# First Gram stage of a delta-rule attention kernel: zero fills and mask casts on ScalarE, sums of squares a step ahead, first keys fetched by two queues

One core of one Trainium2 chip. The metric is the device time of one execution in microseconds (us). All ratios below are the mean time of one kernel's fast runs over the mean of the other's fast runs of the same rounds, so they are not quite the ratios of the medians that stand beside them.

## What is computed

```python
# deltanet: B, H, S, D = 4, 8, 768, 48
k_n = k / (norm(k, axis=-1) + 1e-6)
for t in range(S):
    y[:, :, t] = q[:, :, t] @ state
    v_old = state^T @ k_n[:, :, t]
    state += beta[t] * outer(k_n[:, :, t], v[:, :, t] - v_old)
# then, on x = y as [3072, 384]:
h = x @ w_in                                     # d_ff = 2048
out = (max(h, 0) + alpha * min(h, 0)) @ w_out
```

The kernel cuts the sequence into chunks of 64. A "step" is one such chunk of two of the four sequences, all heads; for each step it needs the products of the keys among each other (the Gram matrices), and for four steps at a time VectorE inverts the resulting triangular blocks ("elimination"). The feed-forward part is TensorE's work and takes most of the time; `alpha` holds its "slopes".

## The kernel before: the parts that matter

```python
def squares(n):                      # sums of squares of the keys of step n
    ksq = work.tile([128, H, D], FP32, name="ksq", bufs=1)
    nc.scalar.square(ksq, early(n)[:, :, 0:D])
    nc.vector.tensor_reduce(out=norm, in_=ksq, axis=AXX, op=ALU.add)

def weigh(n):
    nc.scalar.sqrt(norm, norm)
    nc.vector.tensor_scalar_add(norm, norm, 1e-6)          # L324
    nc.vector.reciprocal(rec, norm)
    nc.gpsimd.tensor_tensor(...)                           # two small products
    ...
def statics(first, last):            # Gram stage of some steps
    for n in range(first, last + 1):
        prep(n)                      # squares(n), weigh(n)
        flips(n, N)                  # transposes of the keys on TensorE
        yield
        ...
            grams(n - 1, N)          # Gram products, evicted by VectorE
...
load_early(0); <load beta>; load_early(1)                  # all on the sync queue
nc.scalar.dma_start(out=al_sb, in_=moe_alpha...)           # the slopes
...
nc.vector.tensor_scalar_mul(minus, above, -1.0)
nc.vector.tensor_copy(out=inside, in_=ones)                # mask cast, 128x1024
...
for t in state + diag + inv + mid:   nc.gpsimd.memset(t, 0.0)
for t in right:                      nc.gpsimd.memset(t[:, 0], 0.0)
...
for _ in statics(0, NJ - 1): pass
slopes()                             # transpose of the slopes, TensorE
for i in range(2): flips(N, i)       # query transposes
busy(BUSY)                           # 32 products that nobody reads: they keep TensorE at work
begin_in(n_in)                       # ScalarE: first halves of the weight conversion
for _ in eliminate(0): pass          # VectorE inverts, about 27 us
```

## Time and profile before

| | before |
|---|---|
| median (lowest to highest), the three runs taken first | 739.37 us (739.34 to 741.58) |
| span in the profile | 737.2 us |
| busy: TensorE, VectorE, ScalarE, GpSimd | 96, 55, 34, 3% |
| first Gram eviction, start | 12.21 us |
| inversion, start | 20.15 us |
| first product with an inverse (L524), start | 49.03 us |

A line of a timeline gives start and length in us, engine, source line, operation, output<-input with sizes, and in brackets the engine's idle time before it and what ended it. A line of the waits gives who waited for whom: us in total, times, longest. The lines of this profile stand in the prediction.

### The profile page before, as it was taken

Reading aid. Unit: us, or ns where it says so; the run is one execution under the profiler, and the core shown is the slowest. Engines: PE = TensorE matmul, PEld = TensorE weight load, DVE = VectorE, ACT = ScalarE, POOL = GpSimd, SP = SyncE. Lnnn points to the kernel's source line nnn. Section 1 sums busy time; section 2 is a strip of 40 time slices with the busy share of each in tenths; the row PEclk is TensorE's granted clock in tenths of the full one; section 3 lists DMA queues with packets and bytes.
Section 4 is the critical chain, followed back from the end, with each engine's and each line's share of the span. In section 5 each row is a group of like instructions: output and inputs, shape, how many; then the busy total and the mean of one; then the engine's idle time right before and its main releaser. Section 6 shows DMA issues by size and latency. Waiting matters only on the chain.

```text
span 737.2 us, 20600 instructions
## 1 busy us (share of the span) xinstructions
PE 706.7 (96%) x8989; PEld 517.7 (70%) x8989; DVE 407.5 (55%) x1041; ACT 247.1 (34%) x564; POOL 23.5 (3%) x88
## 2 busy tenths in 40 slices
PE   5999887789999999999999999999999999999997
PEld 3457765656778678678678678678687687686774
DVE  6996889896986337746247656257554032132120
ACT  3424656514544243144144144134033033131110
POOL 6000000000100000000000000000000000000000
PEclk9999999999999999999999999999999999999999
DMA  6905944212322122122121101201201210100000
GB/s 122 228 26 121 209 142 102 94 22 44 56 58 44 23 45 45 23 44 45 23 44 34 38 20 34 44 12 34 45 18 28 44 33 14 34 2 1 23 1 21
DMA packets 110186, 37.62 MB, mean 51 GB/s; under 512 B 103392, under 2 KB 106480, under 8 KB 110096
## 3 DMA queue, kind: packets, MB, share of 16 engines
q1 hardware_dynamic: 110064, 36.29, 22.5%
q8 instruction: 71, 1.16, 0.6%
q14 instruction: 19, 0.16, 0.1%
q10 hardware_dynamic: 32, 0.01, 0.0%
HBM read 31.56 MB, written 4.72 MB: 49 GB/s over the span
## 4 chain that ended last, share of the span: by engine, by line
PE 80%; DVE 12%; ACT 4%; issue 2%; DMA 1%; POOL 1%; SPq 0%; POOLq 0%; DVEq 0%
PE p_ffn L667 33%; PE p_ffn L637 27%; PE p_ffn L735 5%; PE p_big L567 3%; PE p_big L372 2%; PE p_big L339 2%; PE p_big L594 2%; DVE g L648 2%; PE p_big L524 2%; PE p_big L581 2%; PE p_big L539 1%; PE p_big L610 1%; DVE prod L450 1%; DVE block L456 1%; DVE w_out L213 1%
## 5 line engine op out<-in xcount | busy, mean ns | idle before, releaser
L637 PE MATMUL p_ffn<-xt,w_in 128*128 128x256 f32 x1152 | 269.6, 387 | 9.5 <-DVE g L648 6.2
L667 PE MATMUL p_ffn<-w_out,g 128*128 128x384 f32 x768 | 258.8, 490 | 2.4 <-DVE g L648 2.4
L637 PEld LDWEIGHTS p_ffn<-xt,w_in 128*128 128x128 f32 x1152 | 214.0, 191 | 42.7 <-ACT w_out L201 5.7
L667 PEld LDWEIGHTS p_ffn<-w_out,g 128*128 128x128 f32 x768 | 142.6, 190 | 93.1 <-issue 3.0
L648 DVE SCALAR_TENSOR_TENSOR g<-low,al_t,p_ffn 128x256 f32<-128x256 f32 x192 | 83.5, 476 | 113.9 <-ACT low L645 113.0
L645 ACT ACTIVATE low<-p_ffn 128x512 f32<-128x512 f32 x96 | 57.2, 596 | 114.9 <-PE p_ffn L637 82.3
L673 ACT COPY o_sb<-p_ffn 128x384 f32<-128x384 f32 x24 | 11.5, 479 | 184.0 <-PE p_ffn L667 184.0
L456 DVE TENSOR_TENSOR block<-block,prod 128x30 f32<-128x30 f32 (+9 forms) x180 | 59.7, 332 | 6.2
L450 DVE TENSOR_TENSOR prod<-block 128x30 f32<-128x30 f32 (+9 forms) x180 | 58.8, 327 | 4.0
L570 DVE TENSOR_TENSOR r<-v_raw,p_big 128x384 f32<-128x384 f32 x22 | 12.0, 549 | 79.5 <-PE p_big L567 79.5
L735 PE MATMUL p_ffn<-k_t,ident 128*128 128x512 f32 x78 | 35.9, 606 | 0.0
L601 DVE TENSOR_TENSOR y<-y,p_big 128x384 f32<-128x384 f32 x22 | 12.1, 549 | 40.4 <-PE p_big L594 40.4
L416 ACT COPY same<-right 32x256 f32<-32x256 f32 x40 | 16.1, 402 | 49.3 <-DVE right L381 49.1
L490 ACT ACTIVATE diag<-inverse,which 64x128 f32<-64x128 f32 (+2 forms) x62 | 25.3, 412 | 1.0
L735 PEld LDWEIGHTS p_ffn<-k_t,ident 128*128 128x128 f32 x78 | 14.4, 193 | 15.4 <-issue 15.1
L324 DVE TENSOR_SCALAR norm<-norm 128x8 f32<-128x8 f32 x24 | 6.5, 271 | 30.9 <-ACT norm L323 30.9
L372 PE MATMUL p_big<-k_t 48*64 48x64 f32 x768 | 18.8, 242 | 4.6 <-ACT k_t L361 4.0
L575 ACT COPY y<-p_big 128x384 f32<-128x384 f32 x22 | 10.5, 479 | 34.4 <-DVE r L570 34.4
L372 PEld LDWEIGHTS p_big<-k_t 48*64 48x64 f32 x768 | 15.7, 152 | 8.6 <-ACT k_t L361 5.4
L361 ACT COPY k_t<-p_big 128x512 f32<-128x512 f32 x24 | 13.9, 578 | 23.1 <-PE p_big L339 23.1
L594 PEld LDWEIGHTS p_big<-u,a_t 64*64 64x64 f32 x768 | 13.4, 134 | 11.2 <-issue 8.6
L490 ACT ACTIVATE inv<-inverse,which 128x256 f32<-128x256 f32 x43 | 20.6, 502 | 0.5
(97 smaller groups left out, 638.6 us busy)
## 6 DMA issues: line engine op xcount, KB each, us to landing
w_out<-in_moe_w_in_dram SPq DMA_DIRECT2D x12, 512.0 KB, 5.3
qp<-in_q_dram SPq DMA_DIRECT2D x48, 96.0 KB, 3.0
v_raw<-in_v_dram SPq DMA_DIRECT2D x48, 96.0 KB, 2.9
kl<-in_k_dram SPq DMA_DIRECT2D x96, 48.0 KB, 2.4
out_dram<-o_sb SPq DMA_DIRECT2D x48, 96.0 KB, 2.2
ke<-in_k_dram SPq DMA_DIRECT2D x46, 96.0 KB, 3.1
space_out<-in_moe_w_out_dram SPq DMA_DIRECT2D x11, 384.0 KB, 4.0
w_out<-in_moe_w_out_dram SPq DMA_DIRECT2D x5, 384.0 KB, 3.4
```

Source lines behind the costliest of these rows:

```text
L372: nc.tensor.matmul(p[half(t ^ a if w else t), a, w, g], k_t[n][dims(a), g, half(t)], rhs[n][dims(a), g, half(t)],)
L416: nc.scalar.copy(same[m][own, j], right[n % EARLY][own, 1:])
L450: nc.vector.tensor_tensor(out=prod, in0=r[:, 0:j, j : j + 1].to_broadcast([128, j, n]), in1=r[:, j : j + 1, j + 1 : HB].to_broadcast([128, ...
L456: nc.vector.tensor_tensor(out=r[:, 0:j, j + 1 : HB], in0=r[:, 0:j, j + 1 : HB], in1=prod, op=ALU.add)
L490: nc.scalar.mul(dst[n % NE][to or rows, a.start * G : a.stop * G, cols], src[m][rows, heads], which[rows, i : i + 1],)
L567: nc.tensor.matmul(p[half(t), a, w, g], x[n][dims(a), g, half(t)], state[bp][dims(a), t, g])
L594: nc.tensor.matmul(p[half(t), a, g], a_t[n][half(t ^ a), a * G + g], us[n][half(t ^ a), a, g])
L637: nc.tensor.matmul(p_h[:, i], w_in[:, t, (f + i) * 128 : (f + i + 1) * 128], xt[:, t], start=(t == 0), stop=(t == KT - 1),)
L645: nc.scalar.activation(low, p_h, ACT.Relu, scale=-1.0)
L648: nc.vector.scalar_tensor_tensor(out=g[:, i], in0=low[:, i], scalar=al_t[:, f + i : f + i + 1], in1=p_h[:, i], op0=ALU.mult, op1=ALU.add,)
L667: nc.tensor.matmul(p_o[bp], gs[f // 2][:, f % 2, bp * 128 : (bp + 1) * 128], w_out[:, f], start=(f == 0), stop=(f == FT - 1),)
L735: nc.tensor.matmul(p, ident, k_t[NJ - 1].rearrange("p g i -> p (g i)"))
```

## The change

The intent is to shorten the first stage: take the zero fills from GpSimd and the mask casts from VectorE and put them on ScalarE while VectorE inverts; take the small addition to ScalarE as well; start the reduction of the next step before the present step is finished; and fetch the first keys by two queues. To make room, one of three input buffers is given up for a second squares buffer. The filler grows from 32 to 34 products.

```diff
-BUSY = 32
+BUSY = 34
-    NXT = 3
+    NXT = 2
-    load_early(0)
+    load_early(0, (nc.sync, nc.scalar))
+    load_early(1, (nc.scalar, nc.scalar))
     <load beta on the sync queue>
-    load_early(1)
-    nc.scalar.dma_start(out=al_sb, ...)
...
-    nc.vector.tensor_scalar_mul(minus, above, -1.0)
-    nc.vector.tensor_copy(out=inside, in_=ones)
...
-    for t in state + diag + inv + mid:
-        nc.gpsimd.memset(t, 0.0)
-    for t in right:
-        nc.gpsimd.memset(t[:, 0], 0.0)
+    def zeros():
+        for t in right:
+            nc.scalar.memzero(t[:, 0])
+        for t in mid + diag + inv + state:
+            nc.scalar.memzero(t)
...
-        ksq = work.tile([128, H, D], FP32, name="ksq", bufs=1)
+        ksq = work.tile([128, H, D], FP32, name="ksq", bufs=2)
...
-        nc.vector.tensor_scalar_add(norm, norm, 1e-6)
+        nc.scalar.activation(norm, norm, ACT.Copy, bias=1e-6)
...
     def statics(first, last):
+        if first > 0:
+            squares(first)
         for n in range(first, last + 1):
-            prep(n)
+            if n < last:
+                squares(n + 1)
+            weigh(n)
             flips(n, N)
...
     load_late(0)
+    nc.sync.dma_start(out=al_sb, ...)          # the slopes, now behind 18 other loads
     fetch_in(n_in)
+    squares(0)
+    betas()                                    # the beta transposes, now here
     for _ in statics(0, NJ - 1):
         pass
+    nc.scalar.copy(inside, ones)
...
+    nc.scalar.mul(minus, above, -1.0)
+    zeros()
     busy(BUSY)
```

## The prediction

> **What bounds the kernel now.** I read the page's busy slices first (40 slices of 18.4 us each).
>
> ```profile
> PE   5999887789999999999999999999999999999997
> DVE  6996889896986337746247656257554032132120
> ACT  3424656514544243144144144134033033131110
> ```
>
> TensorE is full from the tenth slice on (about 165 us to the end). Nothing in this change shortens that part. It can only move what comes earlier: the first slice, and the slices from about 74 to 165 us, where TensorE is at seven to nine tenths and VectorE at eight to nine. So I then took the chain of work that ended last for the first 60 us, in order of time (start, length, what):
>
> ```profile
> 5.78 0.69 DVE inside L258
> ...
> 7.17 0.26 DVE beta_t L273
> ...
> 8.29 2.57 DVE norm L324
> ...
> 17.47 1.13 PE p_big L372 x32
> 18.60 0.21 PE p_big L280
> 18.81 1.90 PE p_big L339 x8
> 20.71 27.81 PE p_ffn L735 x64
> 48.52 0.51 issue
> 49.03 2.05 PE p_big L524 x64
> ```
>
> The chain runs through GpSimd's masks, then VectorE's mask cast and betas, then an addition to 8 numbers that lasts 2.57 us, then four Gram steps, then TensorE's filler multiplications (L735: they compute nothing, they only keep TensorE busy while VectorE inverts), and ends in L524, the first product that needs an inverse. From 49.03 on TensorE has no gap until 85 us. So the start of L524 is the number to predict. The filler is not its real cause: 0.51 us of idle stands after it. VectorE's timeline shows the cause:
>
> ```profile
> 8.29 2.56 DVE L324 TENSOR_SCALAR norm<-norm 128x8 f32<-128x8 f32 x1 [0.27 <-ACT norm L323]
> ...
> 11.78 0.17 DVE L324 TENSOR_SCALAR norm<-norm 128x8 f32<-128x8 f32 x1 [0.28 <-ACT norm L323]
> 12.21 0.42 DVE L381 TENSOR_TENSOR same<-p_big,wgt 128x256 f32<-128x256 f32 x1
> ...
> 20.15 2.18 DVE L428 STREAM_TRANSPOSE block<-same 128x256 f32<-128x256 f32 x4
> ```
>
> The same addition costs 0.17 us a step later. The inversion begins at 20.15 and from there needs 49.03 - 20.15 = 28.88 us to L524. The GpSimd timeline says what held the addition:
>
> ```profile
> 8.45 1.00 POOL L290 MEMSET inv<- 128x512 f32 x2
> 9.38 1.00 POOL L290 MEMSET mid<- 128x512 f32 x2
> 10.30 0.52 POOL L294 MEMSET right<- 128x32 f32 x8
> ```
>
> The zero fills end at 10.82 and the addition at 10.85. ScalarE's timeline shows the room for these fills elsewhere: its first weight pieces end at 28.97 and its next work comes after 19.45 us of idle.
>
> ```profile
> 28.29 0.68 ACT L202 ACTIVATE w_out<-w_out 128x512 f32<-128x512 f32 x1
> 48.42 0.91 ACT L490 ACTIVATE diag<-turned,which 128x256 f32<-128x256 f32 x2 [19.45 <-DVE turned L428]
> ```
>
> **What the Trainium skill says.** (1) "SBUF — State Buffer", section "Who interferes with whom": a one-source VectorE operation such as tensor_scalar in a two-port mode and a GpSimd instruction exclude each other, and the later one blocks. The trace agrees: 2.56 us against 0.17, ending with the last fill. (2) "ScalarE: Activation LUTs", section "What ACT_TABLE_LOAD costs": an ACTIVATE with immediate operands takes 186 ns + 0.833 ns per element of the row, and neighbours overlap by 93 ns. The trace has 0.57 to 0.59 us for 512 elements from PSUM (the formula gives 0.61) and 0.66 to 0.69 from SBUF, so it nearly agrees. (3) "DMA: Bandwidth & Descriptors", section "Issuing engines are not separate DMA queues": a second issuing engine saves only the sequencer's time to issue. Here that is 0.65 to 0.72 us for each 96 KB issue on the sync queue, which is not small in the first five microseconds. (4) "TensorE: Matmul & The Clock Gate", section "What's actually happening": the array runs at half clock until it has been busy about 3.4 us. The trace agrees in kind: 32 Gram rows (L372) take 1.13 us before 18.6 us, and 64 of them 1.09 us at 52.14.
>
> **The change part by part.**
>
> *Fills.* Sixteen GpSimd fills (6.82 to 10.82 us) go to ScalarE, behind the query copies. Estimate from point (2): six of 512 elements and two of 384 at about 0.55 and 0.45 us, eight of 32 at about 0.15, the mask negation 0.2: some 5.7 us, plus the cast of `inside`, 1024 elements, about 1.05 us. ScalarE's twelve weight operations then end near 30 us, still 14 us before they are wanted. Free.
>
> *Removed from VectorE's path before the first Gram:* the negation (1.03 us, hidden), the cast (0.69), the blocked addition (2.56, now on ScalarE, no shared port).
>
> *Keys by two queues.* Both halves of the first key are issued at 0.74 us and the beta second instead of third. But the three issues on ScalarE's queue (3 x 0.65) push the table load from 1.15 to about 2.7, so it ends near 4.0 and the first square starts at about 4.2 instead of 4.64. Betas land near 4.2, their transposes end near 5.3, VectorE's four scalings (1.05) end near 6.4, the second reduction 6.95, the first reciprocal 7.1, GpSimd's two products (0.48 in the trace) 7.7. TensorE meanwhile: transposes for beta, two key flips at 1.1 us each, then the first Gram product, 1.13, ends at about 8.7. So the first `same` (12.21 before) comes at about 8.8: 3.4 us earlier.
>
> *Squares a step ahead.* Before, a step was 2.57 us (12.21 to 14.78): 1.4 of Gram evictions and copies, 0.55 reduction, then two waits of 0.28 and 0.2 around the square root, 0.17, 0.2. With the root and the addition long done on ScalarE: 1.4 + 0.55 + 0.18 = 2.13. Steps: 2.13, 1.6, 1.43 (before 2.57, 2.52, 1.43): 1.36 us less, if TensorE keeps up (2.2 us a step at half clock, less if it is warm by then). Inversion start: 8.8 + 5.16 + 1.42 = 15.4, against 20.15: 4.75 us earlier. VectorE would let L524 start at 15.4 + 28.88 = 44.3.
>
> *The filler, grown from 32 to 34.* This is where I expect part of the gain to stop. It is in order on TensorE behind the slopes' transpose (L280) and the query flips. The slopes' input has moved from ScalarE's queue at 0.73 us to the sync queue behind all key, query and value loads. Those issues ended at 14.97; three of 96 KB fewer (1.97) makes 13.0, the small issue 0.4 more, landing (2.6 to 3.3 us for its neighbours, 1.6 for itself before) 15 to 16. From L280 to the filler took 2.11 us, so the filler starts at 17.1 to 18.0, and 34/32 x 27.81 = 29.55 us later it ends at 46.7 to 47.6. Even without that wait, the last flip needs the bank that the last Gram eviction leaves, about 0.6 us before the inversion starts, so the filler ends no sooner than about 45.2. L524 therefore starts at max(44.3, filler's end): about 47 in the first reading. Gain there 2.0 us; 3.8 if the slopes land early; up to 4.7 if VectorE is last.
>
> *Later stages.* From 82 to 160 us the chain runs mostly over VectorE and ScalarE, and TensorE idles about 20 us. Steps 4 to 7 and 8 to 9 there get the early squares as well: per step about 0.27 of wait and 0.2 of addition leave VectorE, 2.5 us in all. ScalarE gets 0.2 more a step. I count 1 us. Two buffers for the feed-forward input instead of three cost nothing: its third use of a buffer comes two chunks later, when the products that read it have been issued. The extra buffer for squares only pays for itself in memory.
>
> Sum: 2.0 to 4.7 early, weighted 2.7, plus 1.0: 739.4 - 3.7, about 735.8.
>
> **The rivals.**
>
> 1. *Filler or slopes become the wait* (my main reading, 55%): 736 to 737. For it: the sum above, and that TensorE is in order. Against it: somebody raised the count to 34, which would be odd if it stood in the way.
> 2. *VectorE stays last* (30%): the whole 4.7 us arrives, plus later gains: 733.5 to 735. It needs the slopes to land before about 14.5.
> 3. *The keys become the wait*: the packets are 192 bytes, and the DMA engines are already at seven to eight tenths between 4 and 13 us. If more issues only queue, the third and fourth keys land no earlier and half the gain goes: 737 to 738 (10%).
> 4. *The gain is lost again between 82 and 160 us*: two windows there (110 to 120 and 140 to 150) show a granted clock of 0.83 after idle TensorE time, so a shift in phase can cost or give a microsecond or two. 737 to 739.5 (5%).
>
> **Range and chances.** The lowest of these is about 733, the highest plausible 738.5. A gain over 2% would need 14.8 us, more than all the TensorE idle before 20 us; a loss over 2% would need a stall that no part of the change makes. Faster 1%, same 98%, slower 1%.
>
> **What the new profile would show.** Right: the 2.56 us addition gone from VectorE; GpSimd idle from about 6.8; first `same` near 8.8 and the inversion near 15.4; the fills on ScalarE between 16 and 24; L524 near 47 with no idle before it, the filler directly ahead of it, and TensorE waiting for the slopes' DMA before L280. Wrong: an idle gap before L524 that ends with VectorE's transposes (rival 2), a square waiting for a key's DMA (rival 3), or an unchanged total with L524 earlier (rival 4).

## The result and the profile after

The changed kernel took 735.21 us (median of 6 runs, 734.64 to 736.87) against 739.23 (6 runs of the kernel before, the three above among them); ratio 0.9946, interval 0.9929 to 0.9964. A later control of the changed kernel in other rounds gave 0.9966 (0.9955 to 0.9976). So it is 0.3 to 0.5% faster, and the predicted 735.8 holds. The way there was not quite the predicted one. The table gives starts from the timelines in us, one trace for each kernel; the last column is a variant that comes below. (The prediction reckoned the filler's start by the chain of waits, which puts it at 20.71 before and 17.95 after.)

| | predicted | before | after | 31 fillers (second run) |
|---|---|---|---|---|
| first Gram eviction | 8.8 | 12.21 | 9.29 | 9.34 |
| inversion | 15.4 | 20.15 | 16.29 | 16.35 |
| first filler row | 17.1 to 18.0 | 20.50 | 17.74 | 17.31 |
| first product with an inverse | about 47 | 49.03 | 47.76 | 45.31 |
| state update of the second step | | 64.15 | 62.70 | 60.38 |
| Gram eviction of step 8 | | 136.42 | 132.05 | 130.45 |
| blocks turned, second elimination | | 167.22 | 162.88 | 161.29 |
| span | | 737.2 | 733.0 | 731.5 |

The gain is 1.3 us at the first product with an inverse, 1.5 at the second state update (62.7), 4.4 at the eviction of step 8 (132) and 4.2 at the end. VectorE's own gain at the start of the inversion, 3.9 us, is mostly lost at the first product. The chain of waits of the changed kernel says why:

```profile
1.57 3.66 DMA space_out<-in_beta_dram
...
12.29 1.11 PE p_big L374 x32
...
15.77 0.25 PE p_big L279
16.03 1.92 PE p_big L341 x8
17.95 29.88 PE p_ffn L737 x68
47.83 1.99 PE p_big L526 x64
```

The filler (L737; 68 rows are 34 products) now runs straight into L526; the half microsecond of idle that stood before L524 is gone. ScalarE's timeline of the changed kernel shows that it had finished the first two diagonal blocks by 45.59, two microseconds earlier:

```profile
6.22 0.53 ACT L315 ACTIVATE ksq<-ke 128x384 f32<-128x384 f32 x1 [1.33 <-DMA ke<-in_k_dram]
...
18.63 1.05 ACT L294 ACTIVATE right<-right 128x32 uint32<-128x32 uint32 x8
19.58 1.14 ACT L296 ACTIVATE mid<-mid 128x512 uint32<-128x512 uint32 x2
...
44.68 0.91 ACT L492 ACTIVATE diag<-turned,which 128x256 f32<-128x256 f32 x2 [13.43 <-DVE turned L430]
```

The fills lie between 18.63 and 23.63 us, beside the inversion, as intended. VectorE's timeline of the changed kernel shows the Gram steps; the blocked addition is gone, and one wait for TensorE has come:

```profile
8.77 0.19 DVE L328 RECIPROCAL rec<-norm 128x8 f32<-128x8 f32 x1
9.29 0.42 DVE L383 TENSOR_TENSOR same<-p_big,wgt 128x256 f32<-128x256 f32 x1 [0.32 <-POOL beta_t L330]
...
13.49 0.42 DVE L383 TENSOR_TENSOR same<-p_big,wgt 128x256 f32<-128x256 f32 x1 [0.50 <-PE p_big L374]
...
16.29 2.26 DVE L430 STREAM_TRANSPOSE block<-same 128x256 f32<-128x256 f32 x4
```

The second part of the gain lies between 62 and 137 us. These are VectorE's waits in 62 to 166 us, first before, then after:

```profile
DVE g L648 <- ACT low L645: 7.4, 8, 1.5
...
DVE norm L324 <- ACT norm L323: 1.9, 7, 0.3
```

```profile
DVE g L650 <- ACT low L647: 7.5, 8, 1.5
...
DVE rec L328 <- ACT norm L326: 0.5, 1, 0.5
```

The wait for the square root fell from 1.9 us in seven places to 0.5 in one, and seven additions of 0.17 us left VectorE.

**How noise looks here.** All runs count as fast, but times of one kernel step by 1.5 to 2 us: in the rounds of the first eight experiments, all on one chip, the kernel before ran between 738.7 and 742.5. The traces show stretches, most of about 3.4 us, in which TensorE is granted half its clock; the one of before has two (around 113 to 117 and 141 to 144 us), the one of after one (around 135 to 139). One such stretch costs the trace 1.7 us of full-speed time.

The fourteen traces show where one such step arises. Behind a wait for VectorE, from about 145 us on, TensorE has a row of 62 feed-forward products. It takes 20.23 us in nine traces and 21.73 to 21.93 in five, and these five are the ones with a half-clock stretch inside it, somewhere between 145 and 156 us. First the changed kernel, then the variant with one queue:

```profile
147.47 20.23 PE L669 MATMUL p_ffn<-w_out,g 128*128 128x384 f32 x62 [2.36 <-DVE g L650]
```

```profile
145.75 21.93 PE L670 MATMUL p_ffn<-w_out,g 128*128 128x384 f32 x62 [2.43 <-DVE g L651]
```

From the eviction of step 8 to the end of the span the nine take 600.7 to 601.1 us and the five 602.5 to 602.7. The five are the variants below with the old order, the additions on VectorE, one queue, the early squares alone, and 28 fillers; their edits share nothing that the traces show as the reason, and the wait before the row (2.38 to 2.43 us in the five, 1.08 to 2.40 in the nine) hardly tells them apart. Why the clock falls there in some executions is not shown. So 1.7 us between two single traces can be this step alone.

So I compare ratios of many runs, the lowest run, and the starts in the traces, and trust a difference most where all three agree.

### The profile page after: what moved, and what is told of

It reads as the page before. It is cut to its first block, busy times and chain, and to the rows that moved or that the text cites. A ratio compares the mean times of both kernels' runs of the same rounds, so it can differ in the third digit from the quotient of the medians.

```text
span 733.0 us, 20599 instructions
## 1 busy us (share of the span) xinstructions
PE 706.1 (96%) x8993; PEld 516.9 (71%) x8993; DVE 400.3 (55%) x1015; ACT 257.9 (35%) x606; POOL 18.1 (2%) x72
## 4 chain that ended last, share of the span: by engine, by line
PE 81%; DVE 11%; ACT 4%; issue 1%; DMA 1%; SPq 0%; DVEq 0%
PE p_ffn L669 33%; PE p_ffn L639 27%; PE p_ffn L737 5%; PE p_big L569 3%; PE p_big L341 2%; PE p_big L374 2%; DVE g L650 2%; PE p_big L596 2%; PE p_big L583 2%; PE p_big L526 2%; PE p_big L541 1%; PE p_big L612 1%; DVE prod L452 1%; DVE block L458 1%; DVE w_out L212 1%
## 5 line engine op out<-in xcount | busy, mean ns | idle before, releaser
L737 PE MATMUL p_ffn<-k_t,ident 128*128 128x512 f32 x82 | 38.0, 611 | 0.0
L737 PEld LDWEIGHTS p_ffn<-k_t,ident 128*128 128x128 f32 x82 | 15.3, 195 | 16.6 <-issue 16.2
L328 DVE RECIPROCAL rec<-norm 128x8 f32<-128x8 f32 x24 | 4.8, 200 | 31.2 <-ACT norm L326 31.1
L363 ACT COPY q_t<-p_big 128x512 f32<-128x512 f32 x24 | 14.0, 588 | 16.5 <-PE p_big L341 16.5
L392 DVE TENSOR_TENSOR a_t<-p_big,minus 128x256 f32<-128x256 f32 x48 | 17.8, 415 | 3.2 <-PE p_big L374 3.2
```

What stands on the lines that cost most here:

```text
L363: nc.scalar.copy(dst.rearrange("p g i -> p (g i)"), src)
L392: nc.vector.tensor_tensor(out=a_t[n_q][:, a * G : (a + 1) * G], in0=p[:, a, 1], in1=minus[:, None, :].to_broadcast([128, G, C]), op=ALU.mult,)
L737: nc.tensor.matmul(p, ident, k_t[NJ - 1].rearrange("p g i -> p (g i)"))
```

## The experiments

Unless it says otherwise, an edit is made to the changed kernel. The first four shared one set of rounds, the next four a second set on the same chip, and the last four, with a control of the changed kernel among them, a third set on another chip. In the first two sets the changed kernel itself was not run again, so its ratio and lowest run there come from other rounds.

### 31 fillers in place of 34

```diff
-BUSY = 34
+BUSY = 31
```

> The changed kernel with 31 filler products in place of 34. Theory (the filler is what TensorE ends last before the first product with an inverse): three fillers of 0.879 us less end at 45.2 us, just when ScalarE has placed the first diagonal block (45.2), so that product starts at 45.2 to 45.4 in place of 47.83, and the whole comes to 732.6 (2.5 us under the changed kernel). Rival (later stages, where VectorE leads, take the gain back): it starts just as early, but the total stays within 1 us of the changed kernel.

Measured: 733.83 us (732.97 to 734.49), ratio 0.9911 (0.9892 to 0.9929). The first product with an inverse came at 46.42, not at 45.2 to 45.4: in this run the inversion itself began at 16.87, 0.6 later, and the first four filler rows ran at half speed (0.86, 0.85, 0.85 and 0.86 us from start to start, then 0.43), so 31 products still just met VectorE. The theory's direction holds and the later stages did not take the gain back: the state update at 61.36 and the end of the span at 731.7 both came 1.3 us earlier than in the changed kernel, like the product itself.

### Slopes loaded behind the beta

```diff
 <load beta on the sync queue>
+nc.sync.dma_start(out=al_sb, ...)
...
-nc.sync.dma_start(out=al_sb, ...)      # behind the key, query and value loads
```

> The changed kernel with the slopes' load issued on the sync queue right behind the beta; 34 fillers. Theory: TensorE's 1.56 us wait before the slopes' transpose is for that load and goes; then the second query flip waits for the bank of the last Gram product (free at 15.63), the filler starts near 16.7 instead of 17.95, and the total falls by 1.2 us. Rival (that wait was for the bank that VectorE frees, as the profile names it): filler still at 17.9, no change in the total.

Measured: 734.18 us (732.65 to 736.13), ratio 0.992 (0.990 to 0.9939). The slopes' transpose began at 12.88 in place of 15.77, straight behind the last Gram product, so the wait was for the load; the rival, the bank that the profile's releaser named, falls. My size was too small: the filler started at 14.56, not near 16.7, since TensorE ran at full speed already from about 10 us, by the length of its products, and the flips took half as long, and the bank's wait did not bind. This early warm-up does not need the edit: the control below (the changed kernel run again) shows it too, and the variant with one queue, which has early slopes as well, does not and starts its filler at 16.32. The first product with an inverse came at 44.52, behind VectorE again:

```profile
41.60 2.31 PE L738 MATMUL p_ffn<-k_t,ident 128*128 128x512 f32 x5
44.52 2.06 PE L527 MATMUL p_big<-diag,right 64*64 64x32 f32 x64 [0.61 <-ACT diag L493]
```

With the slopes early and TensorE warm, 34 fillers end 0.6 us before VectorE is done, as 32 did before the change. Of the 3.2 us at this point 2.2 reached the end of this span.

### The fills alone

The kernel before, with `zeros()` on ScalarE ahead of `busy(BUSY)` and no fills on GpSimd.

> The kernel before with one part of the change: the sixteen zero fills go from GpSimd to ScalarE behind the query copies; everything else, with 32 fillers, as before. Theory (a shared port held by the fills): the first addition takes 0.17 instead of 2.56 us, the first Gram eviction comes at about 9.9 instead of 12.21, the inversion at 17.8 instead of 20.15, the first product with an inverse at 46.7 instead of 49.03, total 736.9. Rival (the addition was long for another reason): it stays at 2.56 us and the total at 739.2.

Measured: 737.14 us (736.95 to 737.25), ratio 0.9955 (0.9938 to 0.9972). VectorE's timeline of this variant:

```profile
8.30 0.17 DVE L324 TENSOR_SCALAR norm<-norm 128x8 f32<-128x8 f32 x1 [0.28 <-ACT norm L323]
8.51 0.20 DVE L326 RECIPROCAL rec<-norm 128x8 f32<-128x8 f32 x1
```

The addition starts at the same time as before and takes 0.17 us instead of 2.56. So it was the fills that held it. The inversion began at 18.40 and L524 at 47.22, a gain of 1.8 us rather than the expected 2.3, because the second square was computed only after the first key copy and then stood in VectorE's way. Lowest run against lowest run (738.83) the total gained 1.9 us.

### Later steps in the old order

```diff
         for n in range(first, last + 1):
-            if n < last: squares(n + 1)
-            weigh(n)
+            if first > 0: prep(n)
+            else: <squares(n + 1) if n < last; weigh(n)>
```

> The changed kernel, with the squares a step ahead kept for the first four steps alone; the later statics (steps 4 to 9) in the old order. Theory (early squares are what brings the 3 us that the changed kernel gains after the first product with an inverse): that gain falls from 3.0 to about 1, total 736.5 to 737.5. Rival (the gain comes from the addition moved to ScalarE, or from phase): total stays within 0.7 of 735.2.

Measured: 739.64 us (738.54 to 740.74, 22 runs), ratio 0.9992 (0.9983 to 1.0). Nearly the whole gain of the change is gone, although the first product with an inverse came at 47.73 as in the changed kernel. I had expected a loss of 1 to 2 us; it is 3.7 to 3.9 by the lowest runs and 1.9 to 3.4 by the ratios (against the control and against the first result). VectorE's waits in 62 to 166 us:

```profile
DVE rec L328 <- ACT norm L326: 3.6, 7, 0.5
DVE norm L317 <- ACT ksq L315: 2.3, 1, 2.3
```

With the addition on ScalarE and no early squares, VectorE waits for two ScalarE operations in each step: 3.6 us against 1.9 before and 0.5 after. The eviction of step 8 came at 135.88, 3.8 us later than in the changed kernel. A further 1.7 us came between the second elimination's turned blocks (166.72) and the next mask product (186.00, against 180.50); that is the step of the long row described above, with a half-clock stretch at 152 to 156 us, and is not to be counted to the order of the squares. The trace has four more such stretches between 87 and 142 us, where the trace of after has one.

### Later additions back on VectorE

```diff
+        if n < NJ:
             nc.scalar.activation(norm, norm, ACT.Copy, bias=1e-6)
+        else:
+            nc.vector.tensor_scalar_add(norm, norm, 1e-6)
```

> The changed kernel, with the addition of 1e-6 given back to VectorE from step 4 on; early squares kept. Theory (the early squares bring the later gain by taking VectorE's wait for the square root away, and the addition's move is a small part): VectorE gets some seven additions of 0.2 us back between 62 and 166 us, total 0.5 to 1.5 us over the changed kernel. Rival (the move of the addition is what helps): total 3 us over it.

Measured: 737.6 us (736.94 to 739.54), ratio 0.9965 (0.9952 to 0.9977). The loss, 2.3 us between lowest runs, lies between the two theories. The part that VectorE's starts show is small: step 8 at 132.58 against 132.05, the turned blocks at 163.36 against 162.88, half a microsecond. The other 1.7 us come between 163 and 181 us, with a half-clock stretch at 149 to 153 us in this trace. That is the long row again (21.93 us), and the one-queue and 28-filler traces show the same 1.7 us with the addition on ScalarE, so the additions are not needed for it. Whether they make it more frequent stays open: against the control of the last rounds (ratio 0.9966) this variant shows no loss at all.

### All keys on one queue again

```diff
-    load_early(0, (nc.sync, nc.scalar)); load_early(1, (nc.scalar, nc.scalar))
+    load_early(0)
     <load beta>
+    load_early(1)
+    nc.scalar.dma_start(out=al_sb, ...)
...
-    nc.sync.dma_start(out=al_sb, ...)
```

> The changed kernel, with all keys on the sync queue and the slopes on ScalarE's queue first, as before the change; 34 fillers. Theory (the second queue gains nothing, since the first Gram product waits for beta, key flips and the first reciprocal at the same times either way): first Gram eviction at 9.2 to 9.6 us against 9.29, and with the slopes early the filler starts by 16.5, total within 0.7 us of the kernel with the early slopes, so 1 us under the changed kernel. Rival (the second queue is worth its 0.5 us or more): first eviction at 9.8 or later, total no lower than the changed kernel.

Measured: 735.1 us (734.44 to 736.64), ratio 0.9931 (0.9916 to 0.9947). The first eviction came at 9.68, between the two theories' figures; the seven traces with two queues and late slopes have 9.22 to 9.86. So the second queue brings at most 0.5 us there and perhaps nothing; one trace with one queue can't settle it. The price of the slopes' new place was larger: with the slopes early the filler started at 16.32 and the first product with an inverse came at 45.98, 1.8 us before the changed kernel's. The total lies 0.8 us over that of the early slopes by the ratios and under the changed kernel, as the theory said.

### Early slopes and 31 fillers

Both edits, the slopes behind the beta and `BUSY = 31`.

> Slopes loaded behind the beta and 31 fillers. Theory: VectorE alone now sets the first product with an inverse (44.5 to 45.3 us), also in runs in which the first filler rows run at half clock, so the total is 732.5 to 733.5 and its spread is smaller than with 34 fillers. Rival (a shorter filler lets TensorE idle and cool): the products after the gap run at half clock and the total is no better than with early slopes alone.

Measured: 735.94 us (733.12 to 741.26, 19 runs), ratio 0.9957 (0.9938 to 0.9976). The rival won. Ten runs lie between 733.1 and 735.9, nine between 738.7 and 741.3, and the mean granted clock of the nine is 0.979 to 0.988 against 0.988 to 0.995 in the ten. The profiled run was one of the nine; for the other eight the same cause is only inferred from their clock and time. TensorE's timeline in it, and after it that of the changed kernel:

```profile
39.52 1.88 PE L738 MATMUL p_ffn<-k_t,ident 128*128 128x512 f32 x4
44.48 3.63 PE L527 MATMUL p_big<-diag,right 64*64 64x32 f32 x64 [3.08 <-ACT diag L493]
48.03 2.07 PE L738 MATMUL p_ffn<-k_t,ident 128*128 128x512 f32 x2
```

```profile
47.76 2.06 PE L526 MATMUL p_big<-diag,right 64*64 64x32 f32 x64
49.75 1.13 PE L737 MATMUL p_ffn<-k_t,ident 128*128 128x512 f32 x2
```

The first product with an inverse starts 3.3 us earlier, but after 3.08 us of idle TensorE. It then takes 3.63 us instead of 2.06, and the granted clock is one half until about 61 us. The second state update comes at 66.98, 4.3 us later than in the changed kernel. In this trace that is what the filler is for, and why a filler that overhangs can be cheaper than one that is too short.

### Early squares in the later steps alone

The kernel before, with `statics` as in the change for `first > 0`, `bufs=2` for the squares and `NXT = 2`.

> The kernel before with one part of the change: squares a step ahead in the later statics (steps 4 to 9) alone, with the second squares buffer and two input buffers; the addition stays on VectorE. Theory: nothing changes before 62 us; VectorE's waits for the square root between 62 and 166 us fall from 1.9 to about 0.5 us, and the total falls by 1.5 to 3 us. Rival (early squares help only together with the addition on ScalarE, or the gain was phase): total within 0.7 us of before.

Measured: 738.32 us (736.54 to 739.55), ratio 0.9966 (0.9952 to 0.998). Nothing changes before 64 us (second state update 64.14). The wait for the square root is 0.3 us in one place. The step-8 eviction comes at 135.09, 1.3 us earlier, and the lowest run is 2.2 us under the lowest of before. By the lowest runs the early squares alone bring a little over half of the change's gain.

A comparison of all traces separates the order of the squares from the clock. From the second state update to the eviction of step 8 the old order takes 72.3 us (before, and the fills alone), and 73.0 with the addition on ScalarE. With early squares it takes 69.4 to 70.2 us in ten traces, and 71.0 here. Among the ten, the five with the addition on ScalarE and no half-clock stretch in that part take 69.4; the four with one or two stretches take 70.0 to 70.2. The trace of before has one stretch there and the trace of after has none. So of the 2.9 us between these two about 2.2 belong to the change and 0.7 to the clock.

### Control, and 31 fillers once more

> The changed kernel unchanged, as a control on the chip and in the rounds of the next three. Both theories: ratio to before 0.994 to 0.996, lowest runs near 734.7 us.

> The changed kernel with 31 fillers, once more, beside the control. Theory (34 overhang what VectorE needs, and 31 leave no gap long enough to cool TensorE): 1.5 to 2.5 us under the control. Rival (the earlier difference was of two chips): within 0.7 us of the control.

Measured: the control 736.92 us (734.89 to 740.21, 22 runs), ratio 0.9966 (0.9955 to 0.9976), a little less than expected. Its trace shows the slopes more plainly than the first one did: the Gram stage was done early, and TensorE stood idle for the load by name.

```profile
16.19 0.20 PE L279 MATMUL p_big<-ident,al_sb 16*128 16x16 f32 x1 [3.02 <-DMA al_sb<-in_moe_alpha_dram]
```

From about 17.3 to 20.8 us the granted clock was then one half, and the first product with an inverse came at 48.30. (All seven traces with late slopes have this wait, of 1.08 to 3.33 us; only that of after names VectorE for it.) With 31 fillers the time was 733.74 us (732.67 to 735.24, 6 runs), ratio 0.9918 (0.9900 to 0.9935). The intervals of the ratios do not touch. The lowest runs differ by 2.2 us. TensorE's timeline with 31 fillers:

```profile
40.59 4.03 PE L737 MATMUL p_ffn<-k_t,ident 128*128 128x512 f32 x9
45.31 2.06 PE L526 MATMUL p_big<-diag,right 64*64 64x32 f32 x64 [0.70 <-ACT diag L492]
```

The product starts 0.7 us after the filler's end, and no half-clock stretch follows up to 95 us. This version beats the kernel before in two separate sets of rounds, and the control in the set in which both ran; of its twelve runs none is above 735.3.

### 28 fillers

> The changed kernel with 28 fillers. Theory (an idle TensorE before the first product with an inverse brings half clock for many microseconds): the filler ends near 43, a gap of 1.5 to 3 us follows, and some runs show the half-clock stretch from 45 to 60 us that 31 fillers with early slopes showed after a gap of 3.08 us; these runs are 4 to 6 us longer, so the runs spread over 733 to 741. Rival (a gap is harmless, the stretch came from elsewhere): all runs within 2 us of the 31-filler kernel, and the first product no later than there.

Measured: 734.87 us (732.79 to 741.46, 20 runs), ratio 0.9948 (0.9927 to 0.997). Nine runs lie between 732.8 and 733.3, three near 735, eight between 738.2 and 741.5; the clock of these eight is 0.982 to 0.988. That is the spread that the theory expected, but none of the eight was profiled, so that a half-clock stretch behind a gap is what made them long is not shown. The profiled run, one of the three, had a gap of 1.29 us before the product at 44.38. The busy times by window show what came next (the last four columns: GpSimd, granted clock, DMA share, GB/s):

```profile
40.00:45.00 5.00, 3.71 (x30) 1.69 (x28) 4.76 (x14) 0.91 (x2) 0.00 (x0) 1.00 0.01 2
45.00:50.00 5.00, 5.00 (x124) 3.75 (x122) 3.19 (x8) 3.23 (x10) 0.00 (x0) 0.69 0.27 71
50.00:55.00 5.00, 5.00 (x98) 3.35 (x96) 3.76 (x9) 0.00 (x0) 0.00 (x0) 0.97 0.09 37
```

From the product to the second state update this run needed 60.85 - 44.38 = 16.5 us; the 31-filler run 60.38 - 45.31 = 15.1. So the gap of 1.29 us went with a loss of 1.4 us in this trace; the clock fell only about 2.5 us after the work had resumed.

### Early slopes and 36 fillers

> Early slopes with 36 fillers: the filler ends between 45.3 us (all rows at full clock) and 47 (first rows at half clock), VectorE is done by 44.5 to 45.3, so no gap. Theory: total 733 to 735, spread under 3 us, better than the control by 1 to 2 us. Rival (the spread comes from later stretches alone): spread as wide as with 34.

Measured: 734.69 us (732.61 to 738.31), ratio 0.9936 (0.9915 to 0.9957). The filler ended at 45.68 and no gap followed. It is better than the control by about 2 us, though the intervals of the ratios just touch, and the spread is 5.7 us and not under 3, as wide as the control's 5.3. So the theory fails for the spread. The rival, that later stretches make it, fits but is not shown: one trace was taken, of a short run, and the long row explains 1.7 us at most.

## Why the prediction was right, and where it was not

The total, the class and the bound were right. The sum was right by luck: two terms were wrong in opposite directions. The early gain was 1.3 us and not 2.7, the later one 2.2 to 2.9 and not 1.0. Of the prediction's own ranges, 736 to 737 for the main reading just missed the first result (735.21) and held the control (736.92).

*The blocked addition* was read correctly, and the fills-only run shows it: 0.17 us against 2.56.

*Keys by two queues* was sized too well. The prediction had the beta land near 4.2 and the first eviction at 8.8. The beta's issue took 0.83 us (0.63 before), its landing came 3.66 us after the issue began, at 5.23, and the second key kept ScalarE waiting until 6.22. The first eviction came at 9.29: 2.9 us earlier, not 3.4. That wait of 1.33 us for a key is the sign that the prediction named for rival 3; it appeared, but the chain at that point ran from the beta over TensorE, and the gain was not halved.

*Squares a step ahead in the first stage*: the steps came out at 2.10, 2.10 and 1.39 us against 2.13, 1.6 and 1.43. The middle one had half a microsecond of wait for TensorE, whose products still took twice their later time (1.11 us for four flips; 0.66 in the control from 11 us on); this was named as a condition and not put into the sum. The inversion started at 16.29 and not at 15.4.

*The filler and the slopes*: the mechanism is shown by four runs (31 fillers twice, early slopes, one queue) and by the control's wait for the load. The slopes' transpose waited 1.56 us for its load, the filler started where predicted, and it ended at 47.8, just past the predicted 46.7 to 47.6, because its first two rows took 0.86 and 0.74 us instead of 0.43. The gain at this point was 1.3 us, where the sum carried 2.7 as a weighted mean. The argument held against this reading, that nobody would raise the count if it stood in the way, has an answer in the runs: 34 is too many here, but with 28 fillers, or with 31 and early slopes, some runs are 4 to 6 us longer.

*Later stages*: the term was mis-sized. "I count 1 us" stood where the text's own working gave 2.5, and the traces show 2.9, of which about 2.2 once the clock is set aside. Taking so little of it was the mistake: nearly all of the time that left VectorE (1.4 us of waits and seven additions of 0.17) came through. The early squares alone gain about 2 us in the total.

*ScalarE's load* was rightly called free: 16 fills, 5.0 us, beside the inversion, and the cast, 1.05, in idle time of ScalarE just before it. Two input buffers instead of three were not tried alone; the run with the early squares alone has that edit too and is faster.

*Slips that changed nothing*: TensorE idles 15.8 us between 82 and 160 us, not about 20; the parts given for the old step add up to 2.8 us and not 2.57, as VectorE's timeline has only one wait of 0.28 in it; six steps of 0.27 and 0.2 make 2.8 us and not 2.5, and the trace has seven.

*What stays open*: why half-clock stretches appear where they do after 80 us, and so how much of the 0.34 to 0.54% in two sets of rounds belongs to the change. In the first stage the fills and the second queue were tried alone; what the moved cast, the earlier beta and the early squares each give there was not.

## What to carry to other kernels

Before shortening a chain, look at what else was sized to its old length: here a fixed filler and a load at the back of a queue took two thirds of a 3.9 us gain, and removing three filler products won 2 us more. A filler must be sized for its worst case in both directions: in single traces a gap of 3.1 us put the second state update 4.3 us behind that of the kernel whose filler overhung by 2 us, while one of 1.3 us went with a loss of 1.4. An operation that is started one step early takes its whole round trip through another engine off an in-order engine, and in this kernel that was worth about 2 us, as much as taking away the visible stall of 2.4.

## What the Trainium skill lacked or had wrong

- "SBUF — State Buffer", section "Who interferes with whom", says that the later instruction blocks for the whole of the first. Here one VectorE addition lasted from 8.29 to 10.85 us, through the whole row of queued GpSimd fills (twelve of them start after it), not through one. The page does not say that a queue of fills can keep the port.
- "TensorE: Matmul & The Clock Gate", section "What's actually happening", gives about 3.4 us of idle time before the clock falls and about 3.4 us of work before it rises. Half-clock stretches followed shorter gaps here, of 3.08 and 1.29 us. And work without a gap did not always raise the clock in that time: in the run with early slopes and 31 fillers the granted clock stayed at one half from 44.48 to about 61 us. In the changed kernel the products from 5.36 to 14.2 us took twice their later time without a gap, although the granted-clock column reads 1.00 there; in that other run they reached full speed at about 10.2. Why is not shown.
- "DMA: Bandwidth & Descriptors", section "Issuing engines are not separate DMA queues", calls the issue time saved by a second queue usually small. For these loads of 96 KB it was about a quarter of the time to land: 0.65 to 0.83 us an issue, and 2.5 us to land for the beta before, 3.66 with two queues. At the first eviction the traces with two queues and late slopes were between 0.5 us earlier and 0.2 later than the one trace with one queue.
- "ScalarE: Activation LUTs", section "What ACT_TABLE_LOAD costs", agreed: two fills of 512 elements took 1.14 us; its formula with the overlap gives 2 x 0.61 - 0.09 = 1.13. The table load took 1.28 us, as the section states.
